# Chunked attention and a gated FFN on one core: scores and value sums as matmuls of one head and chunk on tiles of 64 rows

## The chip, the core and the metric

The kernel runs on one NeuronCore of a Trainium2 chip. The metric is the device time of one execution in microseconds (us), lower is better. The profile is one execution recorded by the hardware. Engines are named as in the profile: PE is TensorE (matmuls; PEld its weight loads), DVE is VectorE, ACT ScalarE, POOL GpSimd, SP SyncE, which issues the DMAs here.

## What is computed

For 4 batches, 8 heads, 768 tokens and a head width of 64, the queries of each chunk of 32 tokens attend to a window of 16 tokens before, the chunk, 8 tokens behind and 8 memory tokens, 64 keys in all. The result goes through an FFN whose hidden layer is gated by the sigmoid of its own convolution over 3 tokens.

```python
for c in range(nc):                                  # 24 chunks of 32 tokens
    k_full = np.concatenate([mem_k, k_ctx], axis=2)  # v_full alike
    scores = scale * np.matmul(q_c, k_full.transpose(0, 1, 3, 2))
    a = np.exp(scores - np.max(scores, axis=-1, keepdims=True))
    a = a / (np.sum(a, axis=-1, keepdims=True) + 1e-09)
    out[:, :, c_start:c_end] = np.matmul(a, v_full)
...
h = np.maximum(x @ w_in, 0.0)                        # 512 -> 1024
for k in range(K):
    conv_out += conv_w[k][None, None, :] * hp[:, k:k + S, :]
gate = 1.0 / (1.0 + np.exp(-conv_out))
return (h * gate @ w_out).astype(np.float32)         # 1024 -> 512
```

The FFN's weights come as 64-bit numbers, which the kernel itself converts.

## The kernel before

**Attention** runs in 32 steps: 4 batches, 2 halves of the sequence, 4 pairs of heads; a step is two heads by 12 chunks. Its host layout puts both heads' 64 dimensions on the 128 partitions. The queries `q_d` hold, for each chunk, 64 columns: the 32 queries of head 0 with zeros in the other head's rows, then those of head 1. So one matmul of `scores` (L481) gives the 64 by 64 scores of one chunk and two heads, on one half of the array's columns; a step has 12, into one PSUM bank `s` (2 buffers). They are float32, and each shows as two MATMUL records in the profile. DVE takes the maximum `top` (L397). Then, by a letter in `SOFT` for each step, V: DVE subtracts (L402) and ACT takes one exponential (L435); A: DVE scales the maximum (L409) and ACT takes six small exponentials (L423); B: as A, with the sums from ACT too, so that DVE's sum `z` (L448) falls away. After the reciprocal (L455) and the scaling of `e` (L459), three 128 by 128 transposes (L502) turn `e` into bank `t`. Two ACT copies (L513) place the two halves of `t` into `a_d`, a block-diagonal array zeroed once at the start (L259), and `values` (L521) multiplies 12 times with `v_t` over all 128 rows into bank `a`. ACT writes the sum's upper part `x_hi` (L530), DVE the remainder `x_lo` (L533): the FFN runs in FP32R in three products.

**FFN.** `ffn_in` (L556) makes, for each of 8 slices of the hidden layer and each half, 12 matmuls of 128 by 384; ReLU follows on ACT (L572). `gate` forms the convolution (first tap L582 on ACT or L586 on DVE by `TAP`, two more on DVE at L592), a sigmoid (L596) and a product (L600, DVE or POOL by `MULT`); `split` makes two FP32R parts (L610, L613, by `LO`). `ffn_out` (L631) sums 24 matmuls of 128 by 512 for each of 6 row tiles a batch. Both use the bank ring `f` of 4 buffers. `from_f64` (L286 to L363) converts the weights in 16 pieces; a letter of `W_IN` or `W_OUT` picks the way (R, S: more on POOL; C, M: more on DVE; a lower-case letter puts one operation, L293, on POOL).

**Order.** Nothing is scheduled on the chip. `Plan` collects all operations with an engine, a cost and a due time from the table `DUE`, and writes each engine's program by a list schedule. Engines then run strictly in that order, and wait at semaphores. One engine, SP, issues all DMAs in order. The 8 PSUM banks are s 2, t 1, a 1, f 4.

Of the kernel before, what the change touches and what calls it, by code (L numbers as in the profile page):

```python
# [32 lines left out]
W_IN, W_OUT = "CrrRcCCm", "rssMCSRs"  # L33
# [184 lines left out]
def attention_then_gated_ffn(  # L218
# [52 lines left out]
    def from_f64(src, hi, lo, key, n, kind, due, first):  # L271
# [9 lines left out]
        def op(eng, cost, do, r, wr, **kw):  # L281
# [90 lines left out]
    def attention(steps, due, soft, norm, zadd):  # L372


        ns = len(steps)
# [1 line left out]
        e = tile_of("e", 2, [P, 2, 2 * NG, KW]) if PAIRS else tile_of("e", 3, [P, 1, 2 * NG, KW])
        top, z = (tile_of(x, 4, [P, 2, 2 * NG]) for x in ("top", "z"))
        part = lambda x, i: x.t[:, i]
        hf = steps[0] % NU // NCC  # L380
        v_of = {}
        for i, n in enumerate(steps):
            b, r = divmod(n, NU)
            cc = r % NCC

            q_d, k_t = (tile_of(*(("h", NFC) if n < 4 else (x, 2)), y) for x, y in (("q_d", [P, NC, 2 * CH]), ("k_t", [P, KC])))
            v_of[n] = v_t = tile_of("v_t", 3, [P, NG, 2, 2, D])
            s = bank("s", 2)
            qk, vd = (lin("qk0", n), lin("v0", n)) if n < 4 else (due[i] - DUE["load"][0], due[i] - DUE["load"][0] + DUE["load"][1])
            load(q_d, q[b, hf, cc], qk, "p c q -> p (c q)")  # L390
            load(k_t, k[b, hf, cc], qk)
            load(v_t, v[b, hf, cc], vd, "p g c h d -> p (g c h d)")
            scores(s, q_d, k_t, due[i])
            s_ = lambda s=s: s.t[:, :W].rearrange("p (g k) -> p g k", k=KW)
            plan.op(
                "V", vec(W), due[i],
                lambda i=i, s_=s_: nc.vector.tensor_reduce(out=part(top, i), in_=s_(), axis=AX.X, op=ALU.max), (s,), ((top, i),),  # L397
            )
            if soft == "V":
                plan.op(  # L400
                    "V", vec(W), due[i],
                    lambda i=i, s_=s_: nc.vector.tensor_tensor(  # L402
                        out=part(e, i), in0=s_(), in1=part(top, i).unsqueeze(2).broadcast_to([P, 2 * NG, KW]), op=ALU.subtract
                    ), (s, (top, i)), ((e, i),),
                )
# [394 lines left out]
```

## Time and profile before

| What | us |
|---|---|
| median of 3 runs (361.95 to 362.36) | 362.33 |
| the profiled execution | 362.77 |
| its span in the trace | 361.1 |
| PE busy / DVE busy / ACT busy / POOL busy | 341.0 / 246.0 / 235.4 / 154.1 |
| mean granted TensorE clock | 0.991 |

The span is what the trace covers; the execution's own time is 1.7 us longer. A busy time is the sum of an engine's instructions, with overlaps counted once. Matmul records overlap, since each one's end is modelled; what a matmul costs is therefore read from the distance between starts, in the timeline.

### The profile page before, as it was taken

What the parts mean: (1) busy time and instruction counts of PE and PEld (TensorE: products, weight loads), DVE (VectorE), ACT (ScalarE), POOL (GpSimd) and SP (SyncE); (2) the same over time, 40 slices, a digit from 0 to 9 for tenths busy, and PEclk for the clock granted to TensorE, in tenths of its full rate; (3) what the DMA queues carried; (4) which work ended last, traced back from release to release, by engine and by line L of the source; (5) the groups of instructions that cost most, each with busy time, mean ns of one, the idle gap of its engine ahead of it and who ended that gap; (6) DMA issues with size and microseconds to landing.
All of it is one profiled execution on the core that took longest, in us unless ns stands there. A gap on an engine that the chain in (4) does not pass through costs nothing.

```text
span 361.1 us, 7615 instructions
## 1 busy us (share of the span) xinstructions
PE 341.0 (94%) x3000; PEld 303.6 (84%) x3000; DVE 246.0 (68%) x395; ACT 235.4 (65%) x504; POOL 154.1 (43%) x188
## 2 busy tenths in 40 slices
PE   0698999999999999999999999999999999999995
PEld 0577999999999988888768899998888799998785
DVE  4989998899999857988951039986523029998200
ACT  5457888878988989897865245688774455452220
POOL 3867556663488356455761001015111104557400
PEclk9969999999999999999999999999999999999999
DMA  8999787975800606205325000023652000000031
GB/s 295 402 344 346 262 317 284 307 249 146 261 13 2 233 0 233 102 3 173 133 87 191 29 32 1 0 62 129 223 197 93 31 29 2 0 0 2 0 116 61
DMA packets 19909, 48.63 MB, mean 135 GB/s; under 512 B 2337, under 2 KB 6689, under 8 KB 19873
## 3 DMA queue, kind: packets, MB, share of 16 engines
q1 hardware_dynamic: 19872, 48.14, 38.7%
q8 instruction: 24, 0.39, 0.5%
q14 instruction: 13, 0.10, 0.1%
HBM read 41.84 MB, written 6.29 MB: 133 GB/s over the span
## 4 chain that ended last, share of the span: by engine, by line
PE 82%; DVE 7%; issue 4%; POOL 3%; DMA 2%; ACT 1%; POOLq 1%; SPq 0%; ACTq 0%
PE f L556 38%; PE f L631 29%; PE a L521 7%; PE s L481 5%; PE t L502 3%; DVE c L592 2%; DMA k_t<-in_k_dram 2%; POOL g L613 1%; POOL c L600 1%; DVE top L397 1%; DVE z L448 1%; POOLq L795 1%; DVE e L459 1%; DVE h L600 0%; DVE e L402 0%
## 5 line engine op out<-in xcount | busy, mean ns | idle before, releaser
L631 PE MATMUL f<-w_out_hi,g 128*128 128x512 f32 (+1 forms) x400 | 127.2, 391 | 0.7 <-POOL g L613 0.7
L631 PEld LDWEIGHTS f<-w_out_hi,g 128*128 128x128 f32 x400 | 74.0, 188 | 17.2 <-POOL g L613 1.2
L556 PE MATMUL f<-x_hi,w_in_hi 128*128 128x384 f32 x256 | 88.1, 344 | 0.0
L556 PE MATMUL f<-x_lo,w_in_hi 128*128 128x384 f32 x256 | 86.1, 336 | 0.0
L556 PE MATMUL f<-x_hi,w_in_lo 128*128 128x384 f32 x256 | 86.1, 336 | 0.0
L631 PE MATMUL f<-w_out_lo,g 128*128 128x512 f32 (+1 forms) x200 | 77.0, 385 | 0.0
L592 DVE SCALAR_TENSOR_TENSOR c<-h,cw,c 128x768 f32<-128x768 f32 x48 | 63.5, 1329 | 6.3 <-ACT c L582 4.9
L556 PEld LDWEIGHTS f<-x_hi,w_in_hi 128*128 128x128 f32 x256 | 48.1, 188 | 1.1
L556 PEld LDWEIGHTS f<-x_hi,w_in_lo 128*128 128x128 f32 x256 | 48.2, 188 | 0.0
L556 PEld LDWEIGHTS f<-x_lo,w_in_hi 128*128 128x128 f32 x256 | 48.1, 188 | 0.0
L572 ACT ACTIVATE h<-f 128x384 f32<-128x384 f32 x48 | 23.4, 493 | 31.9 <-PE f L556 31.5
L631 PEld LDWEIGHTS f<-w_out_lo,g 128*128 128x128 f32 x200 | 37.6, 188 | 7.1
L613 POOL TENSOR_TENSOR g<-c,g 128x768 fp32r<-128x768 f32 x11 | 23.2, 2109 | 37.2 <-ACT g L610 37.1
L513 ACT COPY a_d<-t 64x384 f32<-64x384 f32 x64 | 30.3, 473 | 10.0 <-PE t L502 8.2
L521 PEld LDWEIGHTS a<-a_d,v_t 128*64 128x64 f32 x768 | 26.2, 143 | 9.9 <-issue 4.7
L596 ACT ACTIVATE c<-c 128x768 f32<-128x768 f32 x32 | 27.0, 844 | 10.9 <-DVE c L592 10.7
L643 ACT COPY o_sb<-f 128x512 f32<-128x512 f32 (+1 forms) x25 | 14.0, 574 | 30.2 <-PE f L631 20.8
L521 PE MATMUL a<-a_d,v_t 128*64 128x64 f32 x768 | 30.7, 232 | 2.2 <-ACT a_d L513 2.2
L423 ACT ACTIVATE e<-s,top 128x64 f32<-128x64 f32 (+2 forms) x120 | 29.7, 321 | 2.0 <-DVE top L409 0.9
L459 POOL TENSOR_TENSOR e<-e,z 128x384 f32<-128x384 f32 x26 | 24.4, 940 | 14.8 <-DVE z L455 9.2
L586 DVE TENSOR_SCALAR c<-h,cw 128x768 f32<-128x768 f32 x14 | 15.3, 1092 | 20.7 <-ACT h L572 20.7
L533 DVE TENSOR_TENSOR x_lo<-a,x_hi 128x384 fp32r<-128x384 f32 x32 | 17.6, 551 | 16.3 <-ACT x_hi L530 16.1
(75 smaller groups left out, 495.0 us busy)
## 6 DMA issues: line engine op xcount, KB each, us to landing
v_t<-in_v_dram SPq DMA_DIRECT2D x32, 384.0 KB, 3.4
q_d<-in_q_dram SPq DMA_DIRECT2D x28, 384.0 KB, 4.8
k_t<-in_k_dram SPq DMA_DIRECT2D x28, 252.0 KB, 5.6
out_dram<-o_sb SPq DMA_DIRECT2D x23, 256.0 KB, 2.0
w<-in_w_in_dram SPq DMA_DIRECT2D x8, 512.0 KB, 5.9
w<-in_w_out_dram SPq DMA_DIRECT2D x8, 512.0 KB, 6.0
h<-in_q_dram SPq DMA_DIRECT2D x4, 384.0 KB, 6.8
h<-in_k_dram SPq DMA_DIRECT2D x4, 252.0 KB, 6.5
```

Source lines behind the costliest of these rows:

```text
L423: nc.scalar.activation(part(e, i)[r, g, c], s_()[r, g, c], AF.Exp, bias=part(top, i)[r, g : g + 1], scale=SCALE, accum_out=part(z, i)[r, g ...
L459: lambda i=i: (nc.vector if norm == "V" else nc.gpsimd).tensor_tensor(out=part(e, i), in0=part(e, i), in1=part(z, i).unsqueeze(2).broadcas ...
L481: nc.tensor.matmul(s.t[j * D : (j + 1) * D, o : o + KW], lhsT=q_d.t[:, c], rhs=k_t.t[:, c * STEP : c * STEP + KW], start=True, stop=True,)
L513: nc.scalar.copy(out=a_d[r, :, p, :], in_=t.t[r, : NG * P].rearrange("p (g q) -> p g q", q=CH))
L521: nc.tensor.matmul(a.t[h * D : (h + 1) * D, g * P + j * D : g * P + (j + 1) * D], lhsT=v_t.t[:, g, j, h], rhs=a_d[:, 4 * g + 2 * j + h].re ...
L533: lambda: nc.vector.tensor_tensor(out=x_lo.t[:, cc], in0=a.t[:, :TW], in1=x_hi.t[:, cc].bitcast(F32), op=ALU.subtract),
L556: nc.tensor.matmul(f.t[:, :TW], lhsT=w_in_p[c][:, fc, cc], rhs=x_p[a].t[:, cc], start=(m == 0), stop=(m == 3 * NCC - 1),)
L572: nc.scalar.activation(h.t[:, 1 + o : 1 + o + TW], f.t[:, :TW], AF.Relu)
L592: lambda i=i: nc.vector.scalar_tensor_tensor(out=c.t, in0=h.t[:, i : i + S], scalar=w[i], in1=c.t, op0=ALU.mult, op1=ALU.add), (*H, c), (c ...
L596: plan.op("A", act(S), due, lambda: nc.scalar.activation(c.t, c.t, AF.Sigmoid), (c,), (c,), table="sigmoid")
L613: lambda: (nc.vector if lo == "V" else nc.gpsimd).tensor_tensor(out=g_lo(), in0=x(), in1=g_hi().bitcast(F32), op=ALU.subtract), (h, p[0]), ...
L631: nc.tensor.matmul(ps.t[:, :n], lhsT=g[fc][a].t[:, tt * P : (tt + 1) * P], rhs=w_out_p[c][:, fc, o : o + n], start=(fc == 0 and i == 0), s ...
```

## The change

Scores become matmuls of one head and one chunk: 64 rows (that head's dimensions) by 32 columns of weights, 64 keys moving; 24 a step, on eight tiles of the array (two halves of the rows by four quarters of the columns). A head's scores go to one of two PSUM banks, which alternates with the chunk, so `s` is now one buffer of two banks. The queries have no zeros: their array and its DMA are half as large. The value sums become 24 matmuls of 64 rows by 64 weight columns with 32 columns moving, on four tiles; `a` has two banks. The transposed `e` goes by a single ACT copy into `w_t` (2 buffers); `a_d` and its zeroing are gone. The ring `f` shrinks from 4 to 3. New letters and due times remake the order on all engines, and q and k get rings of 3 and 2.

```diff
-W_IN, W_OUT = "CrrRcCCm", "rssMCSRs"
-TAP = "AAAAAAAAAAAAAAVVVVVVVAAAAVVVVVVV"
-LO = "VVVVGVGGGGGGGGGVVVVGVVVVGVGGGGGG"
-SOFT = "VVVVVVVAVAABBVVAAAABVAAAAAAVBBVB"
-ZADD = "VGGVVVVVGVVVGGGGGGGGGGGGGGGGGGGG"
+W_IN, W_OUT = "CrCCCCCC", "rsScCSCM"
+TAP = "AAVAVVVVVAAAAAAVAAAAVAVVVVVVAAVA"
+LO = "GVVVGVVVVGGGGGGVGVGGGGGGGGGGGGGV"
+SOFT = "VVVVVBAAAAABABBAAAAAABAAVVAAVBVV"
+ZADD = "VGGVGVVGGGGVVGGGVVVVGGVVVGVVGGVV"
...
-    "qk0": (-11.9, 0.47), "v0": (31.6, 0), "late": (-35.7, 0.63), "w_in": (-11.4, 2.51),
+    "qk0": (-13.4, 4.23), "v0": (79, 3.37), "late": (-14.9, 0.27), "w_in": (-22.1, 4.23),
...
-            s = bank("s", 2)
+        s = tile_of("s", 1, [P, 2, 512], pool=psum)
...
             for g in range(NG):
-                for p in range(2):
-                    for j in range(2):
-                        c = 4 * g + 2 * j + p
-                        o = (2 * g + p) * KW
+                for h in range(2):
+                    for w in range(4):
+                        c, r = 4 * g + w, slice(h * D, (h + 1) * D)
                         nc.tensor.matmul(
-                            s.t[j * D : (j + 1) * D, o : o + KW],
-                            lhsT=q_d.t[:, c],
-                            rhs=k_t.t[:, c * STEP : c * STEP + KW],
+                            s.t[w * CH : (w + 1) * CH, h ^ (w & 1), g * KW : (g + 1) * KW],
+                            lhsT=q_d.t[r, c],
+                            rhs=k_t.t[r, c * STEP : c * STEP + KW],
...
-        t, a = bank("t", 1), bank("a", 1)
+        t, a = bank("t", 1), tile_of("a", 1, [P, 2, 512], pool=psum)
+        w_t = tile_of("w_t", 2, [P, NC, CH])
...
-        for p in range(2):
-            r = slice(p * D, (p + 1) * D)
-            def place(r=r, p=p):
-                nc.scalar.copy(out=a_d[r, :, p, :], in_=t.t[r, : NG * P].rearrange("p (g q) -> p g q", q=CH))
-            plan.op("A", act(NG * P, True), due, place, (t,), (("a_d", p),))
+        plan.op(
+            "A", act(NG * P, True), due,
+            lambda: nc.scalar.copy(out=w_t.t.rearrange("p c q -> p (c q)"), in_=t.t[:, : NG * P]), (t,), (w_t,),
+        )
...
-                for j in range(2):
+                for w in range(4):
                     for h in range(2):
+                        c, o = 4 * g + w, h ^ (w & 1)
+                        r = slice(o * D, (o + 1) * D)
                         nc.tensor.matmul(
-                            a.t[h * D : (h + 1) * D, g * P + j * D : g * P + (j + 1) * D],
-                            lhsT=v_t.t[:, g, j, h],
-                            rhs=a_d[:, 4 * g + 2 * j + h].rearrange("p c q -> p (c q)"),
+                            a.t[h * D : (h + 1) * D, w & 1, c // 2 * CH : (c // 2 + 1) * CH],
+                            lhsT=v_t.t[r, c],
+                            rhs=w_t.t[r, c],
...
-        f = bank("f", 4)
+        f = bank("f", 3)
```

On PE the start of the program, ahead of the first FFN matmul, stood like this before (`s` are scores, `t` transposes, `a` value sums; the numbers are buffers, and the first four steps' q and k lie in tiles named `h`):

```order
L481 MATMUL s_135<-h_88,h_86 64x64 x12
L481 MATMUL s_158<-h_92,h_90 64x64 x12
L481 MATMUL s_177<-h_96,h_94 64x64 x12
L481 MATMUL s_200<-h_100,h_98 64x64 x12
L502 MATMUL t_227<-ident_66,e_156 128x128 x3
L521 MATMUL a_243<-a_d_71,v_t_104 64x64 x12
L502 MATMUL t_261<-ident_66,e_190 128x128 x3
L481 MATMUL s_278<-k_t_112,q_d_110 64x64 x12
L502 MATMUL t_294<-ident_66,e_224 128x128 x3
L521 MATMUL a_304<-a_d_71,v_t_106 64x64 x12
L481 MATMUL s_320<-k_t_116,q_d_114 64x64 x12
L521 MATMUL a_354<-a_d_71,v_t_108 64x64 x12
```

Two more scores stood behind these before the FFN began, eight in all. The same place now:

```order
L476 MATMUL s_123<-h_82,h_80 32x64 x24
L476 MATMUL s_159<-h_86,h_84 32x64 x24
L476 MATMUL s_194<-h_92,h_90 32x64 x24
L496 MATMUL t_235<-ident_66,e_154 128x128 x3
L476 MATMUL s_244<-h_100,h_98 32x64 x24
L512 MATMUL a_272<-w_t_241,v_t_102 64x32 x24
L496 MATMUL t_299<-ident_66,e_189 128x128 x3
L476 MATMUL s_318<-k_t_110,q_d_108 32x64 x24
L512 MATMUL a_344<-w_t_312,v_t_104 64x32 x24
L496 MATMUL t_380<-ident_66,e_239 128x128 x3
L512 MATMUL a_394<-w_t_390,v_t_106 64x32 x24
L496 MATMUL t_421<-ident_66,e_310 128x128 x3
```

Scores of a sixth step and the fourth step's value sums follow, and then the first FFN matmul: six scores stand ahead of it. On SP, the first DMAs stood like this before (`w64` are pieces of the FFN's weights):

```order
L286 DMA w64_80<-in_w_in_dram 128x1024
L286 DMA w64_82<-in_w_in_dram 128x1024
L286 DMA w64_84<-in_w_in_dram 128x1024
L471 DMA h_86<-in_q_dram 128x768
L471 DMA h_88<-in_k_dram 128x504
```

And now:

```order
L284 DMA w64_78<-in_w_in_dram 128x1024
L464 DMA h_80<-in_q_dram 128x384
L464 DMA h_82<-in_k_dram 128x504
L464 DMA h_84<-in_q_dram 128x384
L464 DMA h_86<-in_k_dram 128x504
L284 DMA w64_88<-in_w_in_dram 128x1024
```

One piece of the weights, not three, stands ahead of the first q and k, and each q is half as large. The third place is ACT's program just ahead of the ReLU of the first FFN group (`g<-f`), before:

```order
L513 COPY a_d<-t 64x12x32 x2
L348 CAST w_in_hi<-w_top 128x512
L435 ACTIVATE e<-e 128x384
L423 ACTIVATE e<-s,top 128x64 x6
L572 ACTIVATE g<-f 128x384
```

And now:

```order
L503 COPY w_t<-t 128x384
L524 CAST x_hi_306<-a 128x384
L424 ACTIVATE e,z<-s,top 128x64 x5
L424 ACTIVATE e,z<-s,top 32x56
L424 ACTIVATE e,z<-s,top 128x64
L424 ACTIVATE e,z<-s,top 32x56
L346 CAST w_in_hi<-w_top 128x512
L566 ACTIVATE g<-f 128x384
L310 CAST w_in_hi<-w_top 128x512
```

Before, the fourth slice of `w_in` was cast at this place; now the second and third are, behind the eight small exponentials of a step of kind B.

More of the change, by code (lines that the diff above doesn't have):

```diff
@@ L370, in attention_then_gated_ffn, with attention @@
     x_of = {}
[L372 to L375 removed]
+    def attention(n, due, soft, norm, zadd):
         W = 2 * NG * KW
[L377 to L387, printed above, removed]
[L388 to L432 removed]
@@ new lines, in attention @@
+        q_d, k_t = (tile_of(*(("h", NFC) if n < 4 else (x, i)), y) for x, i, y in (("q_d", QB, [P, NC, CH]), ("k_t", KB, [P, KC])))
+        v_t = tile_of("v_t", 3, [P, NC, D])
+        qk, vd = (lin("qk0", n), lin("v0", n)) if n < 4 else (due - DUE["load"][0], due - DUE["load"][0] + DUE["load"][1])
+        load(q_d, q[b, hf, cc], qk, "p c q -> p (c q)")
+        load(k_t, k[b, hf, cc], qk)
+        load(v_t, v[b, hf, cc], vd, "p c d -> p (c d)")
+        scores(s, q_d, k_t, due)
+        plan.op(
+            "V", vec(W), due,
+            lambda: nc.vector.tensor_reduce(out=top.t.rearrange("p g b -> p b g"), in_=s_(), axis=AX.X, op=ALU.max), (s,), (top,),
+        )
@@ new lines, in attention, with less @@
+            plan.op(
+                "A", act(W), due, lambda: nc.scalar.activation(flat(e), flat(e), AF.Exp, scale=SCALE), (e,), (e,), table="exp"
+            )
+        else:
+            plan.op(
+                "V", 150, due,
+                lambda: nc.vector.tensor_scalar(out=flat2(top), in0=flat2(top), scalar1=-SCALE, scalar2=None, op0=ALU.mult),
+                (top,), (top,),
+            )
+            def less():
+                for g in range(NG):
+                    for i in range(2):
+                        todo = [(slice(0, P), slice(0, KW))]
+                        if soft == "B" and hf == 0 and g == 0:
+                            todo.append((slice(0, CH), slice(LEFT, KW)))
+                        if soft == "B" and hf == NH - 1 and g == NG - 1:
+                            todo.append((slice(P - CH, P), slice(0, KW - RIGHT)))
+                        for r, c in todo:
+                            nc.scalar.activation(
+                                e.t[r, g, i, c], s_()[r, i, g, c], AF.Exp, bias=top.t[r, g, i : i + 1], scale=SCALE,
+                                accum_out=z.t[r, g, i : i + 1] if soft == "B" else None,
+                            )
+            plan.op(
+                "A", 6 * act(KW, True, 1) if soft == "A" else 8 * act(KW, True, 2), due, less,
+                (s, top), (e, *((z,) if soft == "B" else ())), table="exp",
@@ L487, in mm, with outcome @@
                         )
[L489 to L495 removed]
+        plan.op("PE", S_NS, due, mm, (q_d, k_t), (s,), mode="rows", late=250)
+    def outcome(b, hf, cc, v_t, e, due):
+        t, a = bank("t", 1), tile_of("a", 1, [P, 2, 512], pool=psum)
+        w_t = tile_of("w_t", 2, [P, NC, CH])
         if (b, hf) not in x_of:
@@ L668, in steps @@
     def steps(i, n):
-        while i < n:
-            size = GROUP[i // 4] == "2" and i % 2 == 0 and 2 or 1
-            attention(range(i, i + size), T_ATT[i : i + size], SOFT[i], NORM[i], ZADD[i])
-            i += size
+        for i in range(i, n):
+            attention(i, T_ATT[i], SOFT[i], NORM[i], ZADD[i])
     def through_gate(b, fc, due, keep=False):
```

128 lines of the change are left out of this document (55 added, 73 removed), and 8 rows, old and new, of the table DUE.

## The prediction

> **What bounds the kernel now.** I read the busy times first, then the chain of waits.
>
> ```profile
> PE 341.0 (94%) x3000; PEld 303.6 (84%) x3000; DVE 246.0 (68%) x395; ACT 235.4 (65%) x504; POOL 154.1 (43%) x188
> PE 82%; DVE 7%; issue 4%; POOL 3%; DMA 2%; ACT 1%; POOLq 1%; SPq 0%; ACTq 0%
> ```
>
> PE is busy for 94% of the span and carries 82% of the chain that ended last. A share over the whole span hides the stages, so next come the busy times by window: bounds, length, busy us (and instructions) of PE, PEld, DVE, ACT and POOL, the granted clock, DMA's share and GB/s. The last row is DVE alone.
>
> ```profile
> 0.00:31.70 31.70, 17.48 (x304) 14.94 (x304) 24.29 (x58) 17.94 (x34) 20.53 (x26) 0.89 0.94 339
> 31.70:100.00 68.30, 68.30 (x821) 64.45 (x819) 63.09 (x137) 58.54 (x149) 38.73 (x55) 1.00 0.79 269
> 100.00:190.00 90.00, 89.17 (x732) 76.22 (x731) 74.61 (x95) 75.13 (x144) 55.86 (x47) 1.00 0.29 97
> 190.00:322.00 132.00, 132.00 (x983) 119.79 (x982) 71.03 (x99) 74.13 (x164) 27.45 (x56) 1.00 0.20 69
> ...
> 0.00:190.00 190.00, 161.99 (x289) 0.98 0.58 199
> ```
>
> From 31.7 us PE does not pause: 68.30 of 68.30, 89.17 of 90, 132 of 132. There a microsecond saved on PE is one gained, as long as the others keep up, and DVE is near: 63.09 of 68.30, and 161.99 of the first 190. The first 31.7 us are another stage: PE half idle, DMA at 94%, DVE at 24.29. What begins and ends it the timeline of PE (start, length, what) and the chain show:
>
> ```profile
> 8.76 3.21 PE L481 MATMUL s<-h 128*64 128x64 f32 x48 [8.76 <-DMA h<-in_k_dram]
> ...
> 25.10 5.61 DMA k_t<-in_k_dram
> 30.70 0.14 issue
> 30.84 0.92 PE s L481 x24
> 31.76 1.25 PE f L556 x6
> ...
> 341.56 14.89 PE f L631 x85
> ```
>
> The first scores wait 8.76 us for a DMA; the first FFN matmul stands behind scores whose keys took 5.61 us to land. PE ends at 356.45 (341.56 + 14.89); 4.7 us of evacuation and output follow.
>
> **What a step costs PE.** Distances between starts, in the timeline:
>
> ```profile
> 39.22 1.57 PE L481 MATMUL s<-k_t,q_d 128*64 128x64 f32 x48
> 40.72 0.44 PE L556 MATMUL f<-x_hi,w_in_hi 128*128 128x384 f32 x1
> ...
> 48.55 0.92 PE L521 MATMUL a<-a_d,v_t 128*64 128x64 f32 x24
> 49.30 0.87 PE L481 MATMUL s<-k_t,q_d 128*64 128x64 f32 x24
> 50.10 0.55 PE L502 MATMUL t<-ident,e 128*128 128x128 f32 x3
> 50.58 0.92 PE L481 MATMUL s<-k_t,q_d 128*64 128x64 f32 x24
> 51.42 0.44 PE L556 MATMUL f<-x_hi,w_in_hi 128*128 128x384 f32 x1
> ...
> 53.73 0.92 PE L521 MATMUL a<-a_d,v_t 128*64 128x64 f32 x24
> 54.58 0.44 PE L556 MATMUL f<-x_hi,w_in_hi 128*128 128x384 f32 x1
> ```
>
> Value sums take 0.85 alone (53.73 to 54.58) and 0.75 with scores of the same tile shape behind them. Scores take 0.80 behind those, 0.84 alone, and two steps' together 1.50 (39.22 to 40.72). So 24 records cost 0.70, or 29 ns each, and a change of tile shape 0.10 to 0.15. A step's scores and sums come to 1.55 as a neighbouring pair and about 1.69 apart; as many stand paired, I take 1.57.
>
> How 24 records come to 0.70 decides the new price. The same row of value sums, counted in windows that all begin at 48.50:
>
> ```profile
> 48.50:48.56 0.06, 0.01 (x2) 0.01 (x2) 1.00 0.81 324
> 48.50:48.64 0.14, 0.09 (x2) 0.09 (x4) 1.00 1.10 446
> 48.50:48.67 0.17, 0.12 (x4) 0.12 (x6) 1.00 0.97 392
> 48.50:48.70 0.20, 0.15 (x4) 0.15 (x6) 1.00 1.01 410
> 48.50:48.73 0.23, 0.18 (x6) 0.18 (x8) 1.00 0.92 374
> ```
>
> Records begin in twos, within 0.01 to 0.03, and the twos some 0.06 apart. So issue is not the limit. With two column tiles, two records per 0.058 fit two tiles that are each held for 0.058.
>
> **The change on PE.** *Scores*: 24 matmuls, 48 records, on eight tiles, each with 64 moving columns as before. If a tile is held for 0.058 and all work together: 48 x 0.058 / 8 = 0.35. If only twos run, as now: 24 x 0.058 = 1.40. *Value sums*: 48 records on four tiles, weights of 64 columns as before, 32 moving instead of 64: 48 x 0.058 / 4 = 0.70 if the weight load holds the tile, 0.35 if the moving columns do; in twos 1.40, or 0.70 with half the columns. I take 0.35 and 0.53, the full use of the tiles, because the two tiles of today's row do work side by side. The two shapes now differ, so each pays its 0.15: 0.50 + 0.68 = 1.18 a step, 0.39 less than 1.57. Some 27 steps lie behind the first FFN matmul: 27 x 0.39 = **-10.5**. Two more scores come to lie there (eight stood ahead of it, six now): 2 x 0.50 = **+1.0**. Transposes stay.
>
> A page of the Trainium skill speaks against it: "TensorEngine Tiling (Array Packing)", Performance Considerations, Instruction Overhead, says that a matmul has about 60 cycles of overhead, and that no tiling should be drawn from a dimension that is already small. By it, an estimate, 48 records at 25 ns would be 1.20 for either group, 390 us in all. The counts above do not bear that out as a limit on issue, since two records begin inside 0.03; they leave it open for a single tile, and the rival in twos below comes to the same end by rows alone.
>
> **The start.** What is loaded first:
>
> ```profile
> q_d<-in_q_dram SPq DMA_DIRECT2D x28, 384.0 KB, 4.8
> k_t<-in_k_dram SPq DMA_DIRECT2D x28, 252.0 KB, 5.6
> ...
> w<-in_w_in_dram SPq DMA_DIRECT2D x8, 512.0 KB, 5.9
> ```
>
> The DMA rows give size and median us to landing. Ahead of the first q and k now stands one 512 KB piece of weights, not three, and q has 192 KB: 0.95 MB instead of 2.1 MB before scores can begin, at the 339 GB/s above some 3 us earlier. DVE has 44 instructions up to the fourth `x_lo` where it had 54, and two scores fewer stand ahead of the FFN; the row of 5.61 us is no longer in front of it. One wait is new: `s` is one buffer, so each of the first scores waits for the subtraction of the one before. Following this order with today's durations I get the first FFN matmul at about 23 instead of 31.7. But the second slice of `w_in` is cast only behind eight small exponentials on ACT, and PE's next FFN group with all that follows waits for it some 3 us. Net **-6**, between -9 and 0 (the 31.7 were DVE's too, not only DMA's).
>
> **DVE, the cover that could go.** Its rows for the first 190 us (busy us, mean ns):
>
> ```profile
> L448 DVE TENSOR_REDUCE z<-e 128x6 f32<-128x384 f32 x21 | 11.6, 553 | 1.1
> L402 DVE TENSOR_TENSOR e<-s,top 128x384 f32<-128x384 f32 x11 | 6.1, 554 | 0.4
> L613 DVE TENSOR_TENSOR g<-c,g 128x768 fp32r<-128x768 f32 x5 | 5.8, 1169 | 0.0
> L409 DVE TENSOR_SCALAR top<-top 128x6 f32<-128x6 f32 x13 | 5.4, 415 | 0.2
> L320 DVE SCALAR_TENSOR_TENSOR w<-w 128x512 uint32<-128x512 uint32 x7 | 5.4, 766 | 0.2
> L293 DVE TENSOR_SCALAR w_top<-w_top 128x512 f32<-128x512 f32 x8 | 5.0, 626 | 0.0
> L315 DVE TENSOR_SCALAR w<-w 128x512 uint32<-128x512 uint32 x7 | 3.4, 479 | 4.4 <-DMA w<-in_w_in_dram 4.4
> L586 DVE TENSOR_SCALAR c<-h,cw 128x768 f32<-128x768 f32 x2 | 1.2, 592 | 0.0
> ```
>
> In the first 16 letters five steps leave V, three to A (0.415 - 0.554) and two to B (0.415 - 0.554 - 0.553): -1.8. Five taps come to DVE: +3.0. Four conversions go from R or S to C or M: 4 x (0.479 + 0.766) = +5.0; four L293 come from POOL: +2.5; two remainders: +2.3. Small ones, such as sums with 1e-9 that go to POOL, about -2. That makes 171 of 162, while PE wants to be through with this part 12 us sooner. DVE's 28 idle us there (190 - 161.99) would have to shrink to about 7; POOL, which has less to do, will slow DVE less. I put **+3** for waits of PE, 0 to +8. ACT loses a copy of 0.47 in each step and gains small exponentials; POOL has room. Three `f` buffers instead of four cost nothing that I can see: three row tiles at a time are what is now opened together.
>
> **Sum.** 361.1 - 10.5 + 1.0 - 6 + 3 = 348.6, with the 1.7 around the span **350**. The profiled execution took 362.77, the median was 362.33; the difference is small beside the rest. The ends: 0.35 + 0.35, a start of -9 and no waits give 339; the same shares with a start of 0 and +8 give 361.
>
> **Rivals.** *In twos (slower).* An f32 matmul makes two records on one tile. If today's twos are these, and not one of each tile, the second holds up all that stands behind it, and more tiles bring nothing: scores 24 x 0.058 = 1.40, sums at least 0.70, so 2.40 a step with the changes of shape. 27 x 0.83 = 22.4, two scores more 3.1, start -6, no waits: 380.6, or **382**; with 1.40 for the sums 401. It turns slower once the groups stream for over 1.34 together. For it: the twos. Against it: the row can be read either way, and 24 records of 64 columns in 0.70 are 29 ns each, while the transposes' three of 128, one after the other on the whole array, take 0.48 less a change of shape, 110 ns each: half as wide would be 55, not 29. The skill's page "TensorE: Matmul & The Clock Gate", Part 3, What overlaps and what doesn't, has matmuls start strictly in order, which this rival needs. *Half the tiles.* Only tiles side by side overlap, or the rows' halves do not: 0.70 + 0.70 + 0.30 = 1.70, +3.5, +1.7, start -6: 360.3, so **362**. *DVE becomes the bound.* It has 171, 7.4 idle ahead of the FFN (31.7 - 24.29) and keeps half of the other 20.6: it ends at 188.7 for 190, only 1.3 gained; eight steps in the second half add 3.1: 356.7, so **358**.
>
> **How the numbers follow.** Forecast 55%, DVE 14%, half the tiles 12%, in twos 19%. The range of 339 to 367 leaves out the twos. A measurement can tell about 0.2% (0.7 us) from no change. Faster: the forecast, DVE and half of the third, 75%; the same 3%; slower 22%.
>
> **What would show it.** Right: the new scores' 48 records in about 0.35 to 0.45 from first to next start, sums about 0.5 to 0.7, the first scores near 5, the first FFN matmul near 23, and DVE about 93% busy to 178. Wrong: 24 twos at 0.058 in either group; PE gaps behind DVE or POOL between 60 and 180; or PE idle behind the weights' conversion at 25 to 45 for more than the 3 us put in.

## The result, and the profile after

The changed kernel takes **374.27 us** (median of 4 runs, 373.2 to 375.9), the kernel before 362.14 beside it (4 runs): a ratio of 1.0345, with a 95% interval of 1.0301 to 1.0388. It is slower, where the prediction said 350 and faster. The profiled execution is the one of 375.9, with a span of 374.0. The profiled executions of runs 1 and 16 below took nearly twice as long as their others (677 and 660 us) and are left out, of the medians too.

The page of the changed kernel, busy times and chain:

```profile
PE 348.5 (93%) x4536; PEld 303.9 (81%) x4536; DVE 254.0 (68%) x412; ACT 231.1 (62%) x504; POOL 142.4 (38%) x171
PE 75%; DVE 12%; ACT 4%; DMA 4%; issue 2%; SPq 1%; POOL 1%; ACTq 0%; POOLq 0%; DVEq 0%
```

PE is still the bound, but its part of the chain fell from 82% to 75%, and DVE, ACT and DMA have grown there. To see where, I cut both executions at the same work: A up to the first FFN matmul, B up to the last FFN-in matmul of the first two batches (the 384th), C up to the first FFN-in matmul of the third batch, D up to PE's last matmul. The busy times by window for these stages (bounds, length, then busy us of PE, PEld, DVE, ACT and POOL, the granted clock, DMA's share, GB/s); the changed kernel:

```profile
0.00:27.30 27.30, 15.03 (x492) 12.22 (x492) 16.70 (x43) 10.77 (x19) 10.07 (x19) 1.00 0.84 293
27.30:139.70 112.40, 103.12 (x1723) 94.78 (x1722) 99.86 (x193) 89.44 (x243) 48.16 (x73) 0.94 0.52 165
139.70:219.10 79.40, 79.40 (x838) 62.87 (x836) 49.86 (x73) 49.91 (x98) 27.51 (x23) 1.00 0.31 99
219.10:370.40 151.30, 150.62 (x1488) 133.95 (x1487) 87.62 (x104) 80.27 (x142) 56.64 (x57) 1.00 0.16 52
```

and the kernel before (its stage A is in the prediction):

```profile
31.70:126.20 94.50, 94.50 (x1050) 90.03 (x1048) 87.52 (x168) 81.79 (x196) 56.82 (x76) 1.00 0.64 216
126.20:206.60 80.40, 79.57 (x576) 64.11 (x575) 51.27 (x68) 58.07 (x112) 38.96 (x31) 1.00 0.32 107
206.60:356.50 149.90, 149.17 (x1077) 134.47 (x1076) 82.95 (x102) 76.92 (x163) 37.75 (x56) 1.00 0.17 57
```

A gained 4.4 us, **B lost 17.9**, C gained 1.0 and D lost 1.4; with 1.0 less behind PE's last matmul that is the 12.9 between the spans (374.0 - 361.1). The whole loss is in B. There PE was never idle before (94.50 of 94.50); now it is idle for 112.40 - 103.12 = 9.3 us, and its granted clock is 0.94, which at 112.4 us is another 6.7. Together 16 of the 17.9. About 1 us more lies at its start: until 29.1 the FFN matmuls still begin 0.32 us apart, and 0.17 later, although the profile gives a clock of 1.00 there.

**What the groups cost.** The timeline of PE of the changed kernel (start, length, what); a group's price is the distance to the next start:

```profile
37.32 0.72 PE L476 MATMUL s<-k_t,q_d 64*32 64x64 f32 x48
37.97 0.44 PE L550 MATMUL f<-x_hi,w_in_hi 128*128 128x384 f32 x1
...
57.19 0.90 PE L512 MATMUL a<-w_t,v_t 64*64 64x32 f32 x48
58.02 0.44 PE L550 MATMUL f<-x_hi,w_in_hi 128*128 128x384 f32 x1
```

Scores cost 0.65 and sums 0.83, together 1.48 a step against 1.57 before and 1.18 forecast. (The 1.57 is between a neighbouring pair and two groups apart; alone, as here, the groups cost 0.84 and 0.85 before, so the scores gained 0.19 and the sums 0.02.) The records of these two groups, counted in windows from one start, the sums first and then the scores:

```profile
57.10:57.25 0.15, 0.06 (x4) 1.00 0.00 0
57.10:57.31 0.21, 0.12 (x8) 1.00 0.00 0
57.10:57.37 0.27, 0.18 (x12) 1.00 0.00 0
57.10:57.88 0.78, 0.69 (x48) 1.00 0.00 0
...
37.20:37.56 0.36, 0.24 (x32) 1.00 0.00 0
37.20:37.85 0.65, 0.53 (x48) 1.00 0.00 0
```

Value sums begin in fours, as many as there are tiles, and the fours 0.06 apart: all 48 records have begun within 0.69. Before, with two tiles, they began in twos 0.06 apart. So four tiles do work side by side, and each is held for 0.06, as long as a tile with 64 moving columns was before: here only 32 columns move, and the 64 columns of weights are what stayed. That the weights hold the tile is a reading; a least time for any short matmul would look the same, and no run parts the two. Of the scores 32 records start in 0.24 and the other 16 take as long again.

**What PE waits for in B.** The longest waits in 27.3 to 139.7 (PE's group, who ended the wait, us in total, times, longest):

```profile
PE a L512 <- DVE x_lo L527: 2.7, 1, 2.7
PE s L476 <- ACT e L424: 1.3, 2, 1.1
PE f L550 <- POOL w_in_lo L356: 1.2, 1, 1.2
PE t L496 <- DVE e L452: 1.0, 1, 1.0
```

Five more, of 0.2 to 0.9, make up the 9: there is no single wait to take away. The timeline around the longest, and the busy times of the stretches with half the clock (second and fourth row) and of the 3.4 us ahead of each:

```profile
46.74 0.90 PE L512 MATMUL a<-w_t,v_t 64*64 64x32 f32 x48
50.31 1.51 PE L512 MATMUL a<-w_t,v_t 64*64 64x32 f32 x48 [2.67 <-DVE x_lo L527]
51.74 0.69 PE L550 MATMUL f<-x_hi,w_in_hi 128*128 128x384 f32 x1
...
52.55 0.52 PE L550 MATMUL f<-x_lo,w_in_hi 128*128 128x384 f32 x1
52.87 0.52 PE L550 MATMUL f<-x_hi,w_in_hi 128*128 128x384 f32 x1
...
58.48 0.34 PE L550 MATMUL f<-x_lo,w_in_hi 128*128 128x384 f32 x1
58.65 0.34 PE L550 MATMUL f<-x_hi,w_in_hi 128*128 128x384 f32 x1
```

```profile
46.35:49.76 3.41, 1.29 (x52) 1.01 (x50) 1.95 (x7) 2.84 (x7) 1.14 (x2) 1.00 1.02 387
49.76:56.58 6.82, 6.27 (x71) 5.78 (x76) 4.08 (x9) 3.83 (x11) 2.03 (x5) 0.50 0.59 199
94.13:97.54 3.41, 2.12 (x105) 1.78 (x98) 3.31 (x9) 3.41 (x11) 0.83 (x1) 1.00 0.79 211
97.54:104.37 6.83, 6.31 (x83) 5.93 (x76) 6.58 (x15) 5.87 (x11) 3.87 (x6) 0.50 0.65 223
```

The sums at 50.31 wait for 2.67 us until the sums of 46.74 have been read from the one `a`, last by `x_lo`; and when PE goes on, FFN matmuls start 0.32 apart instead of 0.17, and the sums take 1.51 instead of 0.90, for 6.8 us, in which the granted clock is 0.50. The same comes again at 97.54, behind waits of 0.51 and 0.78 for a step of attention. Each of the two stretches costs 3.4 us, together the 6.7 above: these waits are paid twice. What `x_lo` waited for, ACT's timeline shows:

```profile
46.92 0.68 ACT L287 ACTIVATE w_top<-w 128x512 f32<-128x512 f32 x1 [2.12 <-DMA w<-in_w_in_dram]
47.51 0.47 ACT L566 ACTIVATE g<-f 128x384 f32<-128x384 f32 x1
47.88 0.66 ACT L353 ACTIVATE w<-w 128x512 f32<-128x512 uint32 x1
48.43 0.48 ACT L566 ACTIVATE g<-f 128x384 f32<-128x384 f32 x1
48.80 0.48 ACT L503 COPY w_t<-t 128x384 f32<-128x384 f32 x1
49.16 0.50 ACT L524 CAST x_hi<-a 128x384 fp32r<-128x384 f32 x1
```

ACT stood 2.12 us at the first touch of a late piece of `w_in` (L287). `x_hi` could read `a` from 47.6 on, when the sums end; it starts at 49.16, since ACT's written order has that piece, two relus, another step for the weights and the copy `w_t` ahead of it. The chain of waits has the piece itself:

```profile
40.32 6.50 DMA w<-in_w_in_dram
```

It was issued at 40, the last three pieces of `w_in` together, behind a k and a q in SP's queue. So the longest wait is explained; the others are not followed to their start here.

### The profile page after: what moved, and what is told of

Read it like the earlier page. It is cut to its first block, busy times and chain, and to the rows that moved or that the text cites. A ratio compares the mean times of both kernels' runs of the same rounds, so it can differ in the third digit from the quotient of the medians.

```text
span 374.0 us, 10698 instructions
## 1 busy us (share of the span) xinstructions
PE 348.5 (93%) x4536; PEld 303.9 (81%) x4536; DVE 254.0 (68%) x412; ACT 231.1 (62%) x504; POOL 142.4 (38%) x171
## 4 chain that ended last, share of the span: by engine, by line
PE 75%; DVE 12%; ACT 4%; DMA 4%; issue 2%; SPq 1%; POOL 1%; ACTq 0%; POOLq 0%; DVEq 0%
PE f L625 35%; PE f L550 28%; PE a L512 6%; PE s L476 4%; DMA w<-in_w_in_dram 3%; PE t L496 3%; DVE c L586 2%; ACT e L424 1%; DVE c L580 1%; DVE top L394 1%; DVE e L452 1%; DVE w L318 1%; DVE z L442 1%; DMA k_t<-in_k_dram 1%; SPq L464 1%
## 5 line engine op out<-in xcount | busy, mean ns | idle before, releaser
L550 PE MATMUL f<-x_hi,w_in_hi 128*128 128x384 f32 x256 | 91.1, 356 | 0.7 <-ACT g L566 0.4
L550 PE MATMUL f<-x_hi,w_in_lo 128*128 128x384 f32 x256 | 88.6, 346 | 2.2 <-POOL w_in_lo L356 1.2
L586 DVE SCALAR_TENSOR_TENSOR c<-h,cw,c 128x768 f32<-128x768 f32 x48 | 60.9, 1278 | 24.1 <-ACT c L576 22.8
L607 POOL TENSOR_TENSOR g<-c,g 128x768 fp32r<-128x768 f32 x16 | 34.9, 2183 | 57.4 <-ACT g L604 57.4
L424 ACT ACTIVATE e<-s,top 128x64 f32<-128x64 f32 (+2 forms) x144 | 36.0, 322 | 5.6 <-DVE top L410 3.4
L512 PEld LDWEIGHTS a<-w_t,v_t 64*64 64x64 f32 x1536 | 28.6, 148 | 12.4 <-issue 4.2
L512 PE MATMUL a<-w_t,v_t 64*64 64x32 f32 x1536 | 32.3, 232 | 4.6 <-DVE x_lo L527 2.7
L594 POOL TENSOR_TENSOR c<-c,h 128x768 f32<-128x768 f32 x12 | 22.0, 1833 | 38.2 <-ACT c L590 36.6
L524 ACT CAST x_hi<-a 128x384 fp32r<-128x384 f32 x32 | 15.5, 485 | 17.6 <-PE a L512 17.5
L604 ACT CAST g<-c 128x768 fp32r<-128x768 f32 x24 | 20.3, 846 | 8.1 <-DVE c L594 5.3
```

The costliest lines, as they stand in the source:

```text
L424: nc.scalar.activation(e.t[r, g, i, c], s_()[r, i, g, c], AF.Exp, bias=top.t[r, g, i : i + 1], scale=SCALE, accum_out=z.t[r, g, i : i + 1] ...
L512: nc.tensor.matmul(a.t[h * D : (h + 1) * D, w & 1, c // 2 * CH : (c // 2 + 1) * CH], lhsT=v_t.t[r, c], rhs=w_t.t[r, c], start=True, stop=True,
L524: plan.op("A", act(TW, True), due, lambda: nc.scalar.copy(out=hi(), in_=sums()), (a,), ((x_hi, cc),))
L550: nc.tensor.matmul(f.t[:, :TW], lhsT=w_in_p[c][:, fc, cc], rhs=x_p[a].t[:, cc], start=(m == 0), stop=(m == 3 * NCC - 1),)
L586: lambda i=i: nc.vector.scalar_tensor_tensor(out=c.t, in0=h.t[:, i : i + S], scalar=w[i], in1=c.t, op0=ALU.mult, op1=ALU.add), (*H, c), (c ...
L594: lambda: (nc.vector if mult == "V" else nc.gpsimd).tensor_tensor(out=y(), in0=c.t, in1=h.t[:, 1 : S + 1], op=ALU.mult), (c, h), (h if kee ...
```

## The experiments

All 18 runs. A ratio is to the kernel before on the same chip, with a 95% interval; A to D are the stages above in us, from PE's starts in each profile (for run 1 see run 13, the same kernel; for run 16 there are none).

| run | kernel | median us | ratio | A | B | C | D |
|---|---|---|---|---|---|---|---|
| | before | 362.1 | | 31.7 | 94.5 | 80.4 | 149.9 |
| | after | 374.3 | 1.030 to 1.039 | 27.3 | 112.4 | 79.3 | 151.3 |
| 1 | before, new tables | 378.1 | 1.038 to 1.051 | | | | |
| 2 | after, old tables | 388.0 | 1.069 to 1.076 | 32.5 | 105.9 | 93.7 | 149.6 |
| 3 | after, old W_IN letters | 381.4 | 1.052 to 1.058 | 33.0 | 109.0 | 82.9 | 151.3 |
| 4 | after, conv_w apart | 378.3 | 1.042 to 1.052 | 27.5 | 111.8 | 82.1 | 151.2 |
| 5 | before, one s | 371.1 | 1.025 to 1.030 | 31.1 | 99.3 | 83.7 | 151.8 |
| 6 | before, three f | 375.1 | 1.036 to 1.042 | 30.5 | 95.7 | 89.9 | 152.5 |
| 7 | after, SOFT all V | 379.1 | 1.047 to 1.053 | 29.1 | 113.8 | 82.0 | 149.6 |
| 8 | new scores, old sums, four f, old tables | 371.9 | 1.026 to 1.032 | 31.1 | 98.6 | 89.3 | 147.6 |
| 9 | before, planner constants | 363.8 | 1.003 to 1.007 | 32.2 | 96.1 | 81.9 | 148.0 |
| 10 | order of 6, four real f | 376.7 | 1.038 to 1.044 | 31.5 | 95.7 | 90.2 | 153.1 |
| 11 | order of 5, two real s | 370.1 | 1.021 to 1.029 | 29.4 | 99.7 | 83.7 | 151.8 |
| 12 | 8 with new tables | 377.7 | 1.041 to 1.048 | 26.4 | 114.0 | 80.2 | 151.9 |
| 13 | 1 once more (one run) | 380.1 | | 33.7 | 96.1 | 98.1 | 146.9 |
| 14 | after, no DVE conversion | 372.3 | 1.023 to 1.038 | 26.5 | 107.5 | 79.3 | 151.4 |
| 15 | after, mixed tables | 382.7 | 1.055 to 1.061 | 32.7 | 115.2 | 78.8 | 152.3 |
| 16 | 8, mixed tables | 369.1 | 1.018 to 1.023 | | | | |
| 17 | 1 with one s | 378.0 | 1.042 to 1.050 | 26.5 | 110.9 | 81.4 | 153.0 |
| 18 | 12 with two s, two f | 393.8 | 1.085 to 1.094 | 31.0 | 102.2 | 105.4 | 148.8 |

### Order or forms (runs 1 and 2)

Run 1 puts the letters, `DUE`, `SWITCH` and `MODE` of the change into the kernel before; run 2 puts those of before into the changed kernel (its diff, in part):

```
-W_IN, W_OUT = "CrCCCCCC", "rsScCSCM"
+W_IN, W_OUT = "CrrRcCCm", "rssMCSRs"
...
-SWITCH, MODE = 69.7, 6.4
+SWITCH, MODE = 74.3, 10.8
```

> The kernel before with only the new letters (W_IN to ZADD), due times, SWITCH and MODE; its matmuls, queries with zeros, two s buffers and four f stay as they were. Theory 'order' (the remade tables, made for other costs, bring the weights and the work of DVE and ACT late, and PE waits for them between 38 and 130 us): about 370 to 376, against 362 of the kernel before. Rival 'forms' (one s of two banks, three f, or the new matmul groups themselves make PE wait): 358 to 363. If both share it: about 366.

> The changed kernel with only the letters, due times, SWITCH and MODE of before; matmul forms, queries without zeros, one s of two banks and three f as changed. Theory 'order': PE saves 27 x 0.08 = 2 us on scores and sums and some 2 to 4 at the start, nothing is lost, so 355 to 360. Rival 'forms': 370 or more, as in the changed kernel (374). If both share it: about 366.

378.1 and 388.0: neither theory alone. Each half of the change is slower by itself than both together. The new forms cost 26 us under the tables of before; the new tables take 13.7 of that back (388.0 to 374.3), and harm the old forms (by 16). The tables are fitted to one plan, and what is open is what in the forms costs 26.

### The weights in B (runs 3 and 4)

Run 3 gives `W_IN` its old letters. Run 4 gives conv_w's words a buffer of their own, so that `w_in` pieces come earlier in SP's queue:

```
-        w = tile_of("w64", W64, [P, WC, 2], U32)
+        w = tile_of("w48", 1, [P, n, 2], U32) if n < WC else tile_of("w64", W64, [P, WC, 2], U32)
```

> The changed kernel with the W_IN letters of before (CrrRcCCm) alone: the conversion of the first weights partly on POOL again, the loads in the same places of SP's queue. If DVE's added work in the conversion is what PE waits for between 38 and 67 us: 364 to 369. If it is the late loads (the last three pieces are issued at 39.84) or the softmax: 372 to 376, as the changed kernel (374).

> The changed kernel with a small buffer of its own for conv_w's words, so that the ring of four w buffers serves the w_in pieces alone: the fourth w_in piece moves ahead of the first v, and the sixth to eighth are issued one by one between the k and q of later steps instead of all three behind them. If the late landing of these pieces (39.84 issued, 46.99 landed) makes the 14 us that are lost between 38 and 67: 361 to 366. If it is the chain of the conversion on DVE and ACT, whenever the pieces land: 371 to 375.

381.4 and 378.3, both slower than the changed kernel and outside every range expected. Run 4 is told best by its timeline of PE and its chain of waits:

```profile
52.28 0.44 PE L550 MATMUL f<-x_hi,w_in_hi 128*128 128x384 f32 x1
...
58.76 0.52 PE L496 MATMUL t<-ident,e 128*128 128x128 f32 x3 [1.41 <-DVE e L452]
...
60.27 1.40 PE L512 MATMUL a<-w_t,v_t 64*64 64x32 f32 x48 [0.34 <-issue]
61.61 0.69 PE L550 MATMUL f<-x_hi,w_in_hi 128*128 128x384 f32 x1
...
63.29 0.52 PE L550 MATMUL f<-x_lo,w_in_hi 128*128 128x384 f32 x1
63.61 0.52 PE L550 MATMUL f<-x_hi,w_in_hi 128*128 128x384 f32 x1
```

```profile
56.56 0.57 DVE top L394
...
57.32 0.59 DVE w_top L304
...
58.05 0.56 DVE e L452
58.61 0.35 DVE w L313
58.99 0.72 DVE w L318
```

The earlier loads do what they should: the seventh FFN-in group starts at 52.28 (the changed kernel 58.02, before 51.4). But the next one starts at 61.61 (before 54.6), behind a row of DVE work for the weights with the attention's own between it, and the slow distances follow again. Here, too, one late thing was taken away and the next stood behind it: B is 111.8 still.

### Buffers (runs 5 to 8)

Run 5, in the kernel before:

```
-            s = bank("s", 2)
+            s = bank("s", 1)
```

Run 6, in the kernel before (`f` in both places that make one, and the second `range` to match):

```
-        f = bank("f", 4)
+        f = bank("f", 3)
...
-    for tt in range(4):
+    for tt in range(3):
```

Run 7 has V for all 32 letters of SOFT in the changed kernel.

> The kernel before, with one s buffer instead of two; all else, matmuls, queries, tables, four f, as before. Theory 'one s': with a single buffer PE, which works strictly in the order written, stands at each step's scores until the subtraction or the small exponentials of the step before have read s; the second run, with the old tables, showed 6.6 us of such waits behind ACT. Then 372 to 380, with waits of L481 for DVE and ACT in the list of waits. Rival 'the groups themselves' (64-row tiles slow PE or what follows them): 361 to 365.

> The kernel before, with three f buffers instead of four and the last FFN matmuls of the first batch in threes, as the change has it; all else as before. If the third f is what lets PE wait (for the relu on ACT that frees it): 368 to 378. If three f are enough, as the prediction took it: 361 to 364.

> The changed kernel with V in all 32 letters of SOFT: DVE subtracts the largest score at once, so that s is free some 0.6 us after the largest is found and not behind six or eight small exponentials on ACT (2 to 3 us); DVE gets up to 10 us more work, ACT less. Theory 'one s': 362 to 370, since what holds s is short. If DVE bounds the first 190 us: 376 to 384. If neither: 372 to 376.

For run 8 the sums of the changed kernel are written as before, on all 128 rows, with the two heads' rows of v put to match the scores' banks:

```
-                            a.t[h * D : (h + 1) * D, w & 1, c // 2 * CH : (c // 2 + 1) * CH],
-                            lhsT=v_t.t[r, c], rhs=w_t.t[r, c],
+                            a.t[h * D : (h + 1) * D, g * P + j * D : g * P + (j + 1) * D],
+                            lhsT=v_t.t[:, 4 * g + 2 * j + h], rhs=a_d[:, 2 * g + j, h::2, :],
...
-        f = bank("f", 3)
+        f = bank("f", 4)
```

> Scores on 64-row tiles and queries without zeros, as changed, with one s of two banks; value sums on full columns of weights with block-diagonal a_d, as before, so that a takes one bank and f has four; letters, due times, SWITCH and MODE of before. Against the second run (388), which has the new sums and three f besides. Theory 'one s': the loss stays, 378 to 388. If the new sums, or three f, make the loss: 355 to 364, faster than before by the start and by 0.15 a step on the scores.

One s costs 9.9 us in the kernel before (371.1 to 361.2), three f 13.9 (375.1). Run 8, at 371.9, lies between its two ranges. Together 23.8, of the 26 that the forms cost in run 2, if they add, which no run shows. And the new scores with four f cost 10.7 (371.9), as one s without them: the 64-row form as such neither gains nor loses what can be seen, and the 0.19 that each step's scores save on PE does not show in the time. So under the tables of before the loss comes with the buffers that the two-bank tiles take away. The two act in different places, as the table shows: one s in B (99.3 for 94.5) and C, three f in C (89.9 for 80.4, of which 2.5 are three scores that come in D before) and D.

V for all letters of SOFT, by which s is given back sooner, is slower still (379.1, B 113.8), with hardly more for DVE to do in B (100.4 us for 99.9). So it is not how long s is held; the order is another in this run too.

### Waits or order (runs 9 to 11)

Run 9 is a control. Runs 10 and 11 keep the plan, and so the order on every engine, of runs 6 and 5, and give the tile back in PSUM:

```
+    def bank(tag, n, real=None):
+        plan.ring(tag, n)
+        return Tile(tag, lambda: psum.tile([P, 512], F32, name=tag, tag=tag, bufs=real or n))
...
-        f = bank("f", 3)
+        f = bank("f", 3, 4)
```

Run 11 has `bank("s", 1, 2)` in the same way.

> A control: the kernel before with only three constants of the planner changed as in the change (the loads' queue free from 950 on, a product on POOL at 2.0 and a maximum at 3 ns an element), which no buffer, tile or letter rests on. If only a change of buffers costs: 361 to 364. If any other order of the same work costs, because the tables were fitted to this one plan: 366 to 372, and the losses of the single edits (9.9 for one s, 13.9 for three f) hold that much that has nothing to do with buffers.

> The kernel of the sixth run (375), with the same order on every engine, planned for three f, but with four f buffers in PSUM. If its 13.9 us are PE's waits on the chip for an f that is still being read: 361 to 365. If they lie in the order that three f force on the plan (fewer row tiles open on each new slice of the gate): 373 to 376, no change.

> The kernel of the fifth run (371), with the same order on every engine, planned for one s, but with two s buffers in PSUM. If its 9.9 us are waits of the scores on the chip for s: 361 to 365. If they lie in the order that one s forces on the plan (scores written late, no step ahead): 369 to 372.

The control moves 0.5% (363.8): this other order costs something, but not 10. And neither buffer, given back, gives back the time: 376.7 for 375.1, 370.1 for 371.1. So under the tables of before the 10 and 14 us are not PE standing on the chip for an s or f that is still read. (At the very start it does stand for s: A is 29.4 in run 11 and 31.1 in run 5; from B on their stages agree within 0.4.) The cost is in **the order that the planner writes** when it has fewer buffers. With three f only three rows of the FFN's output are open to take up each new slice of the gate, and in run 6 the output's matmuls wait 6.0 us in all for such slices, 0.7 in the kernel before. With one s the scores can't be written a step ahead; PE, never idle in B before, is idle there for 3.2 us in run 5, and waits for the copies into `a_d`. Under the new tables no run gave a buffer back in the same order.

### B under the new tables (runs 12 to 18)

Run 12 is run 8 with all tables of the change. Run 14 keeps the order and does nothing at 42 places on DVE:

```
-            plan.op(eng, cost, due, do, r, wr, **kw)
+            skip = eng == "V" and kind == "C" and key[:2] == "in" and kw.get("shared")
+            plan.op(eng, cost, due, (lambda: None) if skip else do, r, wr, **kw)
```

> The changed kernel with its own tables, its scores and one s of two banks, but value sums on full columns as before, so that f has four buffers. By the buffers' theory three f cost some 14 us with the old tables: if they cost as much with the new ones, 358 to 364; if the new tables have been fitted to three f and gave that back, 370 to 378. The sums themselves take 0.85 in place of 0.83 a step, which is nothing here.

> The kernel of the first run once more (old forms, two s, four f, new tables), since its profiled execution of 677 us was disturbed; for its stages. Between the first FFN matmul of the first half and the last of the second batch the kernel before takes 94.5 us and the changed one 112.4. If the new tables make that, old forms with them take 108 to 115 there; if the forms do, 94 to 100, and the 379 are lost elsewhere, at the output of the FFN, for which the tables were made with three f.

> The changed kernel in the same order on every engine, with the six DVE instructions of the conversion left out for the seven w_in pieces of kind C (42 instructions, some 22 us of DVE by the means of their rows; the weights' values are then not what they should be). If DVE's work is what PE waits for between 28 and 140: that stage falls from 112.4 to 95 to 102, and the whole to 358 to 365. If it is the places in the written order, or ACT, POOL and the loads: 105 to 112, and 368 to 374.

Windows of stages B and C of run 13, then B of runs 12 and 14:

```profile
33.70:129.80 96.10, 93.29 (x949) 88.53 (x948) 75.14 (x155) 72.65 (x203) 39.00 (x69) 0.98 0.55 186
129.80:227.90 98.10, 91.45 (x750) 72.02 (x749) 79.32 (x126) 72.50 (x143) 34.60 (x27) 0.97 0.39 129
```

```profile
26.40:140.40 114.00, 101.72 (x1388) 91.65 (x1387) 95.58 (x190) 91.50 (x247) 49.33 (x75) 0.96 0.50 160
```

```profile
26.50:134.00 107.50, 100.23 (x1726) 92.81 (x1722) 83.79 (x160) 88.73 (x243) 47.25 (x73) 0.97 0.54 173
```

The new tables by themselves don't make B long: with two s and four f it is 96.1 (though it then holds less attention work, as counted below). Four f and the old sums don't make it short: 114.0. DVE's conversion work is 4.9 of it at most: in run 14 DVE has 83.79 us to do in B instead of 99.86, and PE is still idle for 7.3 of 107.5, only 2.0 less than in the changed kernel. The rest is mostly the clock, 0.97 for 0.94, and that is in part chance: over the four executions of the changed kernel itself the mean clock goes from 0.981 to 0.991. In all 372.3, which its interval can't tell from the changed kernel. Left were one s and the new form of the scores.

> The kernel of the first run (old matmul forms, four f, the new tables) with one s buffer instead of two. Its first FFN stage took 96.1 us with two s; the changed kernel, which has one, takes 112.4 there, and with four f and the old sums 114.0 (the twelfth run). If one s, together with the new tables, is the cause in that stage: 108 to 116 there, and 388 to 396 in all, since the output of the first batch (98.1) stays. If the scores' new form is: 96 to 100 there, and 378 to 384.

> The kernel of the twelfth run (scores as changed, old sums, new tables) with two s of two banks each and two f in place of four, so that all eight banks are used. If one s is the cause in the first FFN stage: 95 to 101 there instead of 114. If the scores' form or the tables are: 108 to 116. The whole says little, since two f cost in the later stages: 370 to 395.

Run 17 is run 1 with `bank("s", 1)`; run 18 is run 12 with two s of two banks and two f. Windows of B of run 17, then of B of run 18:

```profile
26.50:137.40 110.90, 98.57 (x1028) 90.66 (x1026) 101.98 (x191) 94.70 (x243) 53.28 (x76) 0.97 0.56 182
```

```profile
31.00:133.20 102.20, 95.06 (x1334) 87.87 (x1332) 84.33 (x171) 79.62 (x222) 40.82 (x71) 0.98 0.52 168
```

B as foreseen: 110.9 with one s and the old form, 102.2 with two s and the new one (a point above its range). A and B have to be read together, for with one s six scores stand ahead of the first FFN matmul and with two s eight, and what isn't done in A is done in B. A + B is 129.8 with two s and 137.4 with one (runs 13 and 17), and 133.2 and 140.4 (runs 18 and 12): 7.6 and 7.2 us longer under the new tables, and 4.2 under the old (126.2 and 130.4, before and run 5).

But even A + B does not hold the same work in each, since an order can put a step of attention behind the cut. Counted by PE's records, these groups begin in A and B:

| kernel | scores | transposes | sums |
|---|---|---|---|
| before | 20 | 18 | 18 |
| after, run 12 | 19 | 18 | 18 |
| run 5 | 19 | 17 | 17 |
| run 13 | 18 | 16 | 16 |
| run 17 | 18 | 18 | 17 |
| run 18 | 21 | 16 | 16 |

With the prices of a group alone (scores 0.84 in the old form and 0.65 in the new, transposes 0.48, sums 0.85) the same work can be put beside the same work. By this estimate **one s costs some 6 us up to the end of B under either tables**: 7.6 - 0.48 x 2 - 0.85 = 5.8, 7.2 + 1.3 - 0.96 - 1.7 = 5.8, and 4.2 + 0.84 + 0.48 + 0.85 = 6.4. That is a little under half of the 13.5 by which the changed kernel is behind at that point (139.7 to 126.2). Most of the rest is in the new tables. Run 13 is the kernel before with these alone; it is 3.6 behind there with two scores, two transposes and two sums less, in all 3.6 + 4.3 = 7.9. The new form of the scores makes little of it: runs 12 and 17 differ there by 3.0, of which one score and one sum more are 1.5.

Over the whole kernel run 17 (378.0) is as fast as run 1 (378.1), and not at the 388 to 396 that were expected: with two s the new tables lose as much again in C (98.1 against 81.4), where they were not fitted to two, and where run 13 does attention work that run 17 has behind it.

The two mixed runs set stages A and B by the tables of before, the rest by the new ones (`W_IN`, half of SOFT, NORM and ZADD, 14 of the due times, `SWITCH` and `MODE` of before):

> The changed kernel with the numbers and letters that set the first 130 us (W_IN, the first 16 of SOFT, NORM and ZADD, the due times of attention, FFN-in and w_in) from before, and those that set what comes behind from the change. Stages add: start 32.5 and first FFN 105.9 as in the second run, output of the first batch 79 and the rest 151 as in the changed kernel, in all 368 to 372. If the stages are not independent: 376 to 388.

> Scores as changed with one s, sums as before, four f, and the mixed tables of the run beside it. Stages: 31.1 and 98.6 as in the eighth run, 79 to 82 for the output of the first batch by the new tables, 148 to 151 for the rest, with 5 for the end and what lies around: 361 to 367. The best forms and tables so far; faster than before only if the late steps of attention cost nothing in the third stage. If the stages are not independent: 368 to 378.

382.7: B became 115.2, longer than with either table (105.9 and 112.4). The stages don't add here. Run 16, with four f, came to 369.1, the fastest with the new scores, and still 2% behind the kernel before. No version beat the kernel before.

## Why the prediction was wrong

- **What bounds it** was right: PE, through both executions.
- **Scores and sums, -10.5.** The mechanism was right, and the rivals of twos and of half the tiles are out: eight and four tiles do work together. The size was off. "I take 0.35 and 0.53": the records took 0.53 and 0.69 by the windows above. Sums came out at the 0.70 that the prediction gives for a tile held by its weights; the scores went at the pace of 0.35 for 32 of 48 records only. So a step saves 1.57 - 1.48 = 0.09, and 27 of them 2.4 us: 8 us of the error. The overhead that the prediction quotes from the Trainium skill ("TensorEngine Tiling (Array Packing)", Performance Considerations, Instruction Overhead) would make either group 1.20; these rows do not agree.
- **Two scores moved behind the first FFN matmul, +1.0**: they did, at 0.65 each 1.3.
- **The start, -6.** The first FFN matmul is at 27.3 for 31.7, 4.4 earlier, where "about 23" and a later wait of 3 were forecast. Of that later wait 0.9 came (for POOL's `w_in_lo`, at 32.8). The first scores began at 6.05, near the 5 that was forecast; what was lost between them and the FFN is not settled, though PE was slow there: value sums take 1.43 us (19.64 to 21.07) where they take 0.83 later. And the 4.4 isn't a gain. Run 17 has the FFN at 26.5 with the old queries and scores, against 33.7 in run 13: one s leaves six scores ahead of it instead of eight, and the two come later. Half the bytes of q did nothing that shows: run 8, with the new queries, one s and the old tables, starts at 31.1, and so does run 5 with the old queries.
- **Waits of PE, +3, 0 to +8.** This is the step that failed most. PE's idle time in B is 9.3 us, and the lower clock behind it 6.7: 16. The prediction saw DVE as what PE would wait for, and counted its work; run 14 took some 16 us of that out of B, and B fell by 4.9. Nor did DVE fill up: it was busy for 150.4 of the first 178 us, 84%, where about 93% was forecast. The waits are for single pieces of work in a written order: the longest for `x_hi` on ACT behind a late piece of weights (ACT's timeline above), in run 4 for a row of DVE. The sum has no term for a lower clock behind a wait. The rival "DVE becomes the bound" gave 358 and falls with it.
- **"One wait is new: `s` is one buffer"** was priced at the start alone. There it came: two waits of 1.29 us for DVE's subtraction ahead of the second and third scores. The runs have one s at some 6 us up to the end of B, and at 9.9 in all under the old tables, most of it not as a wait for the buffer (run 11), but by the order.
- **"Three `f` buffers instead of four cost nothing that I can see."** Under the tables of before they cost 13.9. With the new tables C is 79.3; that these pay for it in B, where they are some 8 us behind even in the old forms, is argued and not shown. The Trainium skill, "TensorEngine Tiling (Array Packing)", Restrictions and Gotchas, Gotcha 1, says that row tiles write to different PSUM banks and so press on PSUM; the kernel agrees, with two banks for `s` and two for `a` where one for each buffer was enough. That sentence should have been turned into a term.

The sum in the prediction's own terms: -2.4 for -10.5, +1.3 for +1.0, -4.4 for -6, +16 for +3: +10.5 where -12.5 was forecast, and +12.9 measured between the spans. By the estimate above, the loss up to the end of B is some 6 for one s and some 8 for the new tables.

What stays open: why PE's waits in B fall where they do, step by step, beyond the longest one; and which of the new letters and due times cost the 8 us. Loads and DVE's conversion were taken away singly, not together. And for no form but two were tables at hand that had been fitted to it, so what one s or three f cost at their best is not known.

## What to carry to other kernels

A tile form that takes two banks takes buffers from something else: price each lost buffer, on every stage that uses it, before the matmuls' own gain, and do it by the order that results, since here an order planned for fewer buffers stayed slow with the buffers back. Where an order is fitted to one plan, test an edit under both sets of tables; each half of a change can be slower than the whole. Before two stages are compared, count what work each holds. And a wait of PE can cost more than its length, when the matmuls behind it are slow.

## What the runs showed of the hardware that was not expected

- The granted clock fell to 0.50 for 6.8 us, and FFN matmuls started 0.32 us apart instead of 0.17, without one long pause ahead: in the 3.41 us before, PE had been busy for 1.29 at the first place (changed kernel, 46.35 to 49.76) and for 2.12 at the second (94.13 to 97.54), where no single wait was longer than 0.78. In run 4 it came after waits of 1.41 and 0.34 with transposes and scores between them. The Trainium skill, "TensorE: Matmul & The Clock Gate", Part 1, What's actually happening, has the clock go to half after an idle window of about 3.4 us; half agrees with the distances, but PE was not idle through such a window here.
- Four 64-row tiles with 64 columns of weights and 32 moving columns took 0.06 us for a four, as two 128-row tiles with 64 moving columns took for a two: halving the moving columns gave nothing.
- Eight tiles started 32 records in 0.24 us, 7.5 ns each, but the last 16 of the 48 took 0.27.
